# A new work list for a fused attention and SwiGLU kernel: the order of all pieces, the order of the loads, and who masks in the first batches

## The chip, the cores and the metric

The kernel runs on one core of a Trainium2 chip. Its time is the device time of one execution in microseconds; the number that counts is the median of several runs. TensorE (PE) multiplies, VectorE (DVE), ScalarE (ACT) and GpSimd (POOL) work element by element, and 16 DMA engines move data for queues that SP, ACT and GpSimd feed.

## The reference, cut to what matters

```python
# attention: B, H, S, D = 8, 8, 576, 64, and 16 beacon keys ahead of the 576 others
k_all = np.concatenate([beacon_k, k], axis=2)
v_all = np.concatenate([beacon_v, v], axis=2)
scores = 1.0 / np.sqrt(D) * np.matmul(q, k_all.transpose(0, 1, 3, 2))
causal[:, 16:] = np.triu(np.ones((S, S), dtype=bool), k=1)     # beacons are never masked
scores = np.where(causal, -1000000000.0, scores)
a = np.exp(scores - scores.max(-1, keepdims=True))
attn = np.matmul(a / (a.sum(-1, keepdims=True) + 1e-09), v_all)
# feed-forward on the 4608 tokens, 512 wide, 1536 inside
x = attn.transpose(0, 2, 1, 3).reshape(4608, 512)
g = x @ w_gate
out = (g * (1.0 / (1.0 + np.exp(-g))) * (x @ w_val)) @ w_out
```

## The kernel before

The kernel works in bf16 on data that is float32 in memory; loads from GpSimd's queue convert on the way. The order of all work is written out by hand as a string of letters, `plan` (line 615). `piece` (line 560) takes one letter at a time and issues the instructions of the next piece of that kind. As each engine executes its own instructions in the order in which they were issued, the string fixes the order on every engine and in every DMA queue at once, and semaphores hold back a piece whose data or buffer isn't there.

**Attention** goes by batch (8) and pair of heads (4 in a batch, 32 pairs in all). Every pair has four units of scores, A, B, C and D (`UNITS`, line 42), so a batch has 16 units, u0 to u15 for batch 0, u16 to u31 for batch 1 and so on. The letters:

- `S` (`scores`, line 292) multiplies a unit's keys and queries into PSUM: 2 matmuls, 6 for C. `s` is the same with the causal mask added on TensorE by 4 more small matmuls (8 for C) of the matrix `below`.
- `E` (`exponent`, line 323) is the exponent of the unit on ScalarE, from PSUM into the tile `p`.
- `D` and `M` (`mask`, line 330) set the masked part of a unit to zero after the exponent, for units whose scores were issued with `S`: `D` on VectorE by a multiplication, `M` on GpSimd by `affine_select`; one instruction, two for C.
- `P` and `p` (`pv`, line 348) multiply the weights of a pair with the values: 30 matmuls of 64x65 each. `R` (`normalize`) divides by the sums on VectorE and writes `x`.

Queries and keys of batches 0 to 2 come as long runs (`run_loads`) and are turned on TensorE: `c` or `C` regroups on VectorE or ScalarE, `T` transposes on TensorE, `K`/`k` and `Q`/`q` copy the result on VectorE or ScalarE. Those of batches 3 to 7 come in row blocks (`kl`, `ql`), and SP turns them by DMA: `t` is one such transpose (`dma_transposes`, line 272), ten for each batch, alternately of a block of keys and of queries. Values (`vl`) come in six loads a batch. All these tiles exist twice, for even and odd batches; `p` exists three times.

**From attention to the feed-forward part** `x` is transposed to `xT`: for batch 0 on TensorE (`X`, with `Y`/`y` to copy), for the others by five or six DMA transposes of SP (`V`, `x_transpose`, line 392).

**Feed-forward** goes by tiles of 512 tokens (9) and 12 blocks of 128 inner columns. `G` and `H` (`gate_value`, line 404) are 8 matmuls of 64x512 each: the first and second half of gate and value. `g` does the very first block in parts (`parts`, line 557). `a` is a tanh on ScalarE, `1` and `2` are two VectorE instructions that make the gated block. `F` (`project`, line 444) is one step of the output projection, 2 matmuls; `O`/`o` (`evacuate`, line 469) copies 128 finished rows on VectorE or ScalarE and stores them through SP's queue. Weights (`weights`, `load_wo`) are loaded in blocks of columns: `weights[0]` and `[1]` are gate and value for inner blocks 0 to 2, `[2]` and `[3]` for 3 to 5, and so on.

**Buffers and queues.** PSUM is cut into four slots of two banks; each T, S, P, G, X and pair of output blocks takes the next free one (`take`, line 101) and gives it back after its last reader. `l` issues the next load of the list `loads` (line 541) on GpSimd's DMA queue, so loads and `M` masks stand in one line on GpSimd. SP's queue holds `t`, `V` and the stores. `h` orders two idle matmuls (`keep_warm`, line 139) ahead of the next scores or P.

Of the kernel before, what the change touches and what calls it, by code (L numbers as in the profile page):

```python
# [55 lines left out]
def kernel(  # L56
# [112 lines left out]
    def runs(b, src, h0, h1):  # L169
        base = HALF * (src is q)  # L170
        return nc.gpsimd.dma_start(
            qk[b % 2][base : base + HALF, RUN * h0 : RUN * h1].rearrange("p (h e) -> p h e", e=RUN),
            src[b, h0:h1].rearrange("h (p i) d -> p h (i d)", i=ROWS),
        )
# [9 lines left out]
    def q_loads(b):  # L184
        return [lambda c=c, n=n: rows(natural(b, 0), q, b, c, 0, P * c, n) for c, n in enumerate((P, P, P, P, 64))]
# [7 lines left out]
    def k_loads(b):  # L193
        return key_loads(natural(b, 1), k, beacon_k, b)

    def v_loads(b):
        return key_loads(vb[b % 2], v, beacon_v, b)

    def run_loads(b):
        return [lambda: runs(b, k, 0, H), lambda: runs(b, q, 0, H)]  # L200

    def beacon_load(b):
        return nc.gpsimd.dma_start(
            beacons[b][0:NB, :].rearrange("j (h d) -> j h d", d=D), beacon_k[b].rearrange("h j d -> j h d")
        )

    def w_loads(i):
        cols = slice(384 * i, 384 * i + 384)
        return [
            lambda t=t, src=src: nc.gpsimd.dma_start(  # L210
                t[:, :, cols], src[:, cols].rearrange("(kk p) f -> p kk f", p=P)
            )
            for t, src in ((wg, moe_w_gate), (wv, moe_w_val))
        ]

    def load_wo(i):
        fs = slice(6 * i, 6 * i + 6)
        nc.gpsimd.dma_start(wo[:, fs, :], moe_w_out.rearrange("(f p) e -> p f e", p=P)[:, fs, :])
# [53 lines left out]
    def dma_transposes(b):  # L272
        def one(is_k, c, n):
            nc.sync.dma_start_transpose(  # L274
                (qT, kT)[is_k][b % 2][:, :, P * c : P * c + n],
                qk[b % 2][0:n, QK * is_k + H * D * c : QK * is_k + H * D * c + H * D],
            )

        todo = []
        for c in range(NKT):  # L280
            todo.append(lambda c=c: one(1, c, P if c < 4 else 80))
            todo.append(lambda c=c: one(0, c, P if c < 4 else 64))
        return todo
# [246 lines left out]
    for i in range(2):  # L530
# [6 lines left out]
    weights = [load for i in range(4) for load in w_loads(i)]  # L537
    vl = [v_loads(b) for b in range(B)]
    kl = [k_loads(b) for b in range(B)]
    ql = [q_loads(b) for b in range(B)]  # L540
    loads = [
        vl[0][3], vl[0][4], vl[0][1], lambda: beacon_load(1), vl[0][2], vl[0][0], vl[0][5], run_loads(1)[1],
        run_loads(1)[0], weights[0], weights[1], weights[4], weights[2], weights[3], weights[7], vl[1][0],
        vl[1][4], weights[5], run_loads(2)[0], vl[2][0], vl[1][5], vl[1][3], weights[6], vl[1][2], vl[1][1],
        lambda: load_wo(0), lambda: beacon_load(2), lambda: load_wo(1), run_loads(2)[1], ql[3][1], ql[3][4],
        vl[2][4], kl[3][0], kl[3][3], vl[2][1], vl[2][2], kl[3][5], vl[3][2], kl[4][0], ql[3][2], kl[3][2],
        vl[2][5], vl[3][0], vl[2][3], kl[4][2], ql[3][0], vl[3][4], ql[3][3], ql[4][2], kl[4][5], kl[4][3],
        kl[3][1], ql[4][4], vl[3][3], kl[3][4], kl[4][1], ql[4][1], vl[3][1], ql[4][3], kl[4][4], ql[4][0],
        vl[3][5], kl[5][0], kl[5][1], ql[5][0], kl[5][2], ql[5][1], kl[5][3], ql[5][2], kl[5][4], ql[5][3],
        kl[5][5], ql[5][4], vl[4][0], vl[4][1], vl[4][2], vl[4][3], vl[4][4], vl[4][5], kl[6][0], kl[6][1],  # L550
        ql[6][0], kl[6][2], ql[6][1], kl[6][3], ql[6][2], kl[6][4], ql[6][3], kl[6][5], ql[6][4], vl[5][0],
        vl[5][1], vl[5][2], vl[5][3], vl[5][4], vl[5][5], kl[7][0], kl[7][1], ql[7][0], kl[7][2], ql[7][1],
        kl[7][3], ql[7][2], kl[7][4], ql[7][3], kl[7][5], ql[7][4], vl[6][0], vl[6][1], vl[6][2], vl[6][3],
        vl[6][4], vl[6][5], vl[7][0], vl[7][1], vl[7][2], vl[7][3], vl[7][4], vl[7][5],
    ]
    turns = [load for b in range(NPE, B) for load in dma_transposes(b)]
    parts = [(0, [(0, 0), (1, 0), (1, 1), (0, 1)], False), (0, [(0, 2), (1, 2)], False), (0, [(1, 3), (0, 3)], True)]
    wholes = 1

    def piece(kind):  # L560
# [52 lines left out]
    skipped = [0]  # L613

    plan = [
        "0lTlkQlhhhhscEslTKlEsQlEslcEhhscTlKTqlQklEslEsllEsEhshhhhhPlplEsRPEsplXRESEYhhsXEMsYPElscpEcsTRE",
        "TlqKhhPXqKpySlRESgcEMSXclgEYMTgQkMTGaKlqG12SHElDSaGE1H2lGaDl1SHEl2HaDGl1a2G1SHE2HlalG1aM2G1lSHE2",
        "lSaHME1lG2laGD1lSHE2HaDG1a2SHE1lP2alSpDESRMPEp1MSFEFRFFlFFSF2ESMFFFPEMFFpMFlRPFFpcFlFRTFFqFKFVFF",
        "FcFSFOoTESFKFFFEQSFFFcESFFcTFDMElTQFklFSKFEFSlFQFFESMDFFFFMESFMOlGoDlEGlDSHlEGlaDS1HlE2HlaG1Mal2",
        "Gl1SHE2lHlaDG1al2Gl1SHlE2GlaD1Hl2Glat1PlH2tlpaGlRtHl1Gta2H1t2Ga1tSHE2HtaDS1FaFtFE2FFFF1FtSP2EFFD",  # L620
        "ptMSPREFFMtpPRFFtpFRFlSFtESlFFFFlEDSVFFFlFEDSFOFFlFEOSFESlDFFFDFEMSPlFEFpMSFlRFESFEFMFDFSFlESPtF",
        "MFEDlpGtRlGlDtlSHElGtaM1Hlt2Halt1Gal2FFtF1GOoSH2EHaDG1a2G1SHE2HaMlG1al2Gl1SHE2lHlaG1aM2Gl1SHlEt2",
        "GaMtl1SHEl2tHaMSl1FatFFlE2FFFF1tFMSP2EFFtpMSPREFtFpDSlFREStFlFFFEDSlFVFFFEMSFFlFFEDSFloFDPoFlFpE",
        "SFRFESFFFDFEMSFPFEDSpEDSFRtFFESFFDPtEDGDpGRFFFSFEtFlFHDlOoGla1SHlEt2HlaDtGl1a2Glt1SlHE2tHlatGM1a",
        "l2Glt1SHE2tHaDG1ta2Gt1SHE2GaD1SHE2HaDG1a2G1SHE2HaDS1aFFF2EFFF1SFEFF2FFPDFPDppRlSFlEFFFRVSlFESFFD",
        "lFFEDSFFlFFEOSFMoFFFESlFFFMFESMFFFESDPFFEpDSMRPtEFFpDStGREFFMtGSHtEHaDtG1a2FtFH1G2ta1Gt2HGta1Ht2",
        "Ha1Ga2FFF1G2FHOoGa1SHE2MGa1SHE2HaMG1a2G1SHE2HaDS1aFFF2EFFF1SFEFMF2FFPDFPppRlSFlEFFFRVSlFESFFDlFF",
        "ESFFlFFESFloFFFoMDFFMFESFFFFEMSPFEMSpFRFEMSFFEFFDSFMEGGMSHEHaMG1a2FFH1G2a1G2HGa1H2Ha1Ga2FFH1OoGa",
        "2G1SH2EMHa1Ga2G1P2HpaGRH1Ha2S1aFFFEF2FFF1FSF2ESFFDPEDSFpFEDSFESRFFFFESDVFFDFFEDSFFFOFEFFFOFFFDFF",
        "FDFPPppRSFEFFFRSFESFFDPEMSFpFEMRGGDPHpaHRFaFF1VGOoG2H1G2a1H2Ga1H2Ga1H2Ga1H2Ga1H2Ga1H2Ga1H2Ga1FFF",  # L630
        "F2FHGa1H2Ha1Ga2FFH12Ga1G2HGa1FH2Ha1Ga2FFF1G2FHGa1FFFF2FFFFFFFFFoOFFFFFFFFFFFHGa1FFFF2FFFHGa1H2Ha",
        "1Ga2FFF1G2FFHOoGa1H2Ga1FFFF2FFHGa1H2Ha1Ga2FFH12Ga1G2HGa1FFFF2HGa1H2FaFFG1F2FHGa1H2FaFFG1F2FFFFOF",
        "FFFOFFFFFFHGa1H2FaH1FaFF2FFF1FFF2FFFFOFFFFOFFFFFFFFFFFFFFFFFFFFOoFFFFFFFFFFFOFFFFFOFFFFFFFoO",
    ]
    for kind in "".join(plan):
        piece(kind)
# [38 lines left out]
```

## Time and profile before

| | us |
|---|---|
| median of 3 runs | 386.75 (386.39, 386.75, 388.0) |
| the profiled execution | 386.35 |
| its span, first to last instruction | 384.6 |
| TensorE, matmuls busy | 358.7 |
| VectorE busy | 231.5 |
| ScalarE busy | 183.6 |
| GpSimd busy | 123.8 |
| DMA, bytes moved | 39.9 MB |

The span is what lies between the first and the last instruction on the core; the execution's time is 1.75 us more. In the profile's slices each digit is the busy share of one fortieth of the span, 9.6 us. A group of instructions, a line of a timeline or a wait names the engine, the line of the code, the operation and the tiles (out<-in). "Issue" as the end of a wait means that the engine waited for nothing that the profile shows. All matmuls are issued through the helper `halves`, so they carry line 132 and are told apart by their tiles: gv_ps is G and H, o_ps is F, s_ps is S, pv_ps is P and p, t_ps is T, xt_ps is X. GpSimd's masks are line 340, its loads lines 171 to 218; line 274 is `t`, line 397 is `V`.

### The profile page before, as it was taken

To read this page: it belongs to the slowest core of one execution; us is meant where nothing else is said; L and a number is where in the kernel's file an instruction comes from. 1 tells how busy PE (TensorE), PEld (TensorE's weight loads), DVE (VectorE), ACT (ScalarE), POOL (GpSimd) and SP (SyncE) were. 2 spreads that over 40 slices of the span, in tenths; PEclk is the share of its full clock that TensorE was granted. 3 is DMA by queue.
4 is the path that set the end of the run, shared out by engine and by line. 5 is a ranking of instruction groups with operands and counts; after the bars stand their busy time and mean duration, and the time that the engine had idled before them with its cause. 6 is when DMAs were issued, how large, how long until landed. Compare 5 with 4: busy or idle time off the path is not lost.

```text
span 384.6 us, 12123 instructions
## 1 busy us (share of the span) xinstructions
PE 358.7 (93%) x5314; PEld 205.6 (53%) x5314; DVE 231.5 (60%) x424; ACT 183.6 (48%) x266; POOL 123.8 (32%) x200
## 2 busy tenths in 40 slices
PE   6768999999969999679998999999999999999996
PEld 3554556555636456445565556555674555555543
DVE  4473877857834676237863776187737765566552
ACT  2873665663537457526565456734733332232110
POOL 8932663499147386641042004400010000000000
PEclk9896999999989999989999999999999999999999
DMA  8999999899999999999439723901134000110112
GB/s 152 154 204 194 140 201 71 93 201 145 143 116 171 127 162 131 136 164 178 65 34 185 90 70 30 155 3 56 30 91 103 16 2 8 48 56 0 58 56 110
DMA packets 143989, 39.90 MB, mean 104 GB/s; under 512 B 130368, under 2 KB 139328, under 8 KB 143936
## 3 DMA queue, kind: packets, MB, share of 16 engines
q0 software_dynamic: 95424, 18.85, 65.8%
q1 hardware_dynamic: 48224, 19.92, 28.8%
q8 instruction: 41, 0.67, 0.8%
q10 hardware_dynamic: 288, 0.36, 0.3%
q14 instruction: 12, 0.10, 0.1%
HBM read 38.27 MB, written 9.44 MB: 124 GB/s over the span
## 4 chain that ended last, share of the span: by engine, by line
PE 83%; DMA 5%; DVE 4%; issue 4%; ACT 2%; SPq 2%; DVEq 0%
PE gv_ps L132 47%; PE o_ps L132 22%; PE pv_ps L132 7%; PE s_ps L132 6%; DMA xT<-x 2%; DMA first<-in_k_dram 1%; SPq L274 1%; DMA qT<-qk 1%; DVE u L429 1%; DVE o_sb L224 1%; DVE x L373 1%; ACT o_sb L222 1%; DVE turn L224 1%; PE t_ps L130 1%; DVE kT L224 0%
## 5 line engine op out<-in xcount | busy, mean ns | idle before, releaser
L132 PE MATMUL gv_ps<-xT,wg 64*128 64x512 bf16 x864 | 199.6, 377 | 1.7 <-DMA xT<-x 0.7
L132 PE MATMUL gv_ps<-xT,wv 64*128 64x512 bf16 x864 | 200.4, 378 | 0.0
L327 ACT ACTIVATE p<-s_ps 128x992 bf16<-128x992 f32 (+2 forms) x128 | 106.3, 866 | 70.1 <-PE s_ps L132 69.4
L132 PE MATMUL o_ps<-wo,hT 64*128 64x512 bf16 (+2 forms) x912 | 115.7, 370 | 0.2
L132 PEld LDWEIGHTS <-wg 64*128 64x128 bf16 x864 | 80.1, 94 | 45.7 <-PE gv_ps L132 2.6
L429 DVE SCALAR_TENSOR_TENSOR u<-th,gv_ps 128x512 f32<-128x512 f32 x108 | 73.9, 684 | 49.5 <-ACT th L425 49.3
L425 ACT ACTIVATE th<-gv_ps 128x512 f32<-128x512 f32 x108 | 64.4, 596 | 82.4 <-PE gv_ps L132 82.4
L132 PEld LDWEIGHTS <-wv 64*128 64x128 bf16 x864 | 79.7, 94 | 41.4 <-issue 1.5
L436 DVE SCALAR_TENSOR_TENSOR hT<-gv_ps,u 128x512 bf16<-128x512 f32 x108 | 74.6, 691 | 3.6
L340 POOL TENSOR_SCALAR_AFFINE_SELECT p<-p 128x256 bf16<-128x256 bf16 (+2 forms) x65 | 24.8, 398 | 128.2 <-ACT p L327 120.7
L132 PEld LDWEIGHTS <-hT 64*128 64x128 bf16 x912 | 47.4, 95 | 34.3 <-issue 1.4
L132 PE MATMUL s_ps<-qT,kT 64*128 64x80 bf16 (+4 forms) x384 | 46.6, 288 | 7.1 <-DMA qT<-qk 2.4
L132 PE MATMUL pv_ps<-vb,p 64*128 64x65 bf16 x1920 | 41.0, 193 | 9.5 <-issue 9.3
L132 PEld LDWEIGHTS <-p 64*128 64x128 bf16 x1920 | 38.0, 96 | 18.9 <-issue 10.9
L132 PEld LDWEIGHTS <-kT 64*128 64x128 bf16 x384 | 22.6, 96 | 24.9 <-issue 10.8
L180 POOL DMA_DIRECT2D vb<-in_v_dram x40 | 34.3, 869 | 3.5 <-DMA qk<-in_q_dram 1.7
L336 DVE TENSOR_TENSOR p<-p,upper 128x256 bf16<-128x256 bf16 (+2 forms) x77 | 19.7, 276 | 26.0 <-ACT p L327 25.8
L372 DVE RECIPROCAL rec<-pv_ps 128x10 f32<-128x10 f32 x32 | 7.0, 219 | 42.9 <-PE pv_ps L132 42.7
L373 DVE TENSOR_TENSOR x<-pv_ps,rec 128x640 bf16<-128x640 f32 x32 | 26.4, 825 | 1.1
L224 DVE COPY o_sb<-o_ps 128x512 f32<-128x512 f32 (+2 forms) x22 | 14.0, 657 | 16.5 <-PE o_ps L132 13.5
L222 ACT ACTIVATE o_sb<-o_ps 128x512 f32<-128x512 f32 (+1 forms) x16 | 9.0, 580 | 29.8 <-DVE o_sb L224 22.6
L180 POOL DMA_DIRECT2D qk<-in_k_dram x25 | 21.5, 873 | 2.7 <-DMA vb<-in_v_dram 2.4
(52 smaller groups left out, 112.4 us busy)
## 6 DMA issues: line engine op xcount, KB each, us to landing
out_dram<-o_sb SPq DMA_DIRECT2D x34, 256.0 KB, 2.7
vb<-in_v_dram POOLq DMA_DIRECT2D x24, 128.0 KB, 6.6
qk<-in_q_dram POOLq DMA_DIRECT2D x20, 128.0 KB, 7.1
qk<-in_k_dram POOLq DMA_DIRECT2D x15, 128.0 KB, 7.5
wg<-in_moe_w_gate_dram POOLq DMA_DIRECT2D x4, 384.0 KB, 13.4
wv<-in_moe_w_val_dram POOLq DMA_DIRECT2D x4, 384.0 KB, 15.8
wo<-in_moe_w_out_dram POOLq DMA_DIRECT2D x2, 768.0 KB, 11.5
qk<-in_q_dram POOLq DMA_DIRECT2D x2, 576.0 KB, 8.7
```

Of the source, the lines that this page charges most:

```text
L132: ins = nc.tensor.matmul(o, lhsT=l, rhs=r, start=start, stop=stop)
L180: return nc.gpsimd.dma_start(dst[p0 : p0 + n, c, :, 0:D], src[b, :, r : r + n, :].rearrange("h j d -> j h d"))
L222: nc.scalar.activation(o, i, ACT.Copy)
L224: eng.tensor_copy(o, i)
L327: nc.scalar.activation(pt[n // 4 % NPT][:, :, c0 : c0 + w], ps[:, :, 0:w], ACT.Exp, scale=0.125)
L336: nc.vector.tensor_tensor(out=ap, in0=ap, in1=upper[:, None, d : d + w].to_broadcast([P, 2, w]), op=ALU.mult)
L340: nc.gpsimd.affine_select(out=ap, in_=ap, compare_op=ALU.is_ge, fill=0.0, base=d, pattern=[[0, 2], [1, w]], channel_multiplier=-1,)
L372: nc.vector.reciprocal(rec[:], o[:, :, :, D : D + 1])
L373: nc.vector.tensor_tensor(out=xs[b][:, :, P * m : P * m + P].rearrange("p c (h d) -> p h c d", d=D), in0=o[:, :, :, 0:D], in1=rec[:].to_br ...
L425: nc.scalar.activation(th[:], gvs[n][0][:, 0, :], ACT.Tanh, scale=0.5)
L429: nc.vector.scalar_tensor_tensor(out=u[:], in0=ths[n][:], scalar=1.0, in1=gvs[n][0][:, 0, :], op0=ALU.add, op1=ALU.mult)
L436: nc.vector.scalar_tensor_tensor(out=hTs[j][:, f, :], in0=gvs.pop(n)[0][:, 1, :], scalar=0.5, in1=ths.pop(n)[:], op0=ALU.mult, op1=ALU.mult)
```

## The change

Three things are edited; all functions stay as they are.

- `plan` is composed anew. In batches 0 and 1 no unit is masked on GpSimd any more (11 units before): 22 units are masked on TensorE (15 before) and 10 on VectorE (6 before). In later batches 48 units are masked on GpSimd (40 before) and 48 on VectorE (56 before). `h` appears 10 times (16 before). The last scores of batch 3 come earlier against the feed-forward work, those of batches 4 to 7 stand elsewhere too; each kind of feed-forward letter appears as often as before. Two evacuations move from VectorE to ScalarE, and some of the copies `K`, `Q` and `Y` change between the two.
- `loads` is in another order. For batches 3 and 4 keys and queries now come in their natural order, block by block, each batch by itself, then the values of batch 3; before, they were interleaved. In the first part one block of weights comes ahead of the values of batch 0.
- `parts`, the very first gate and value block, is done in two parts (6 and 2 steps) and not three (4, 2 and 2).

The old lines of `loads` and `plan`, which stand in the code above, are left out here.

```diff
@@ -539,22 +539,22 @@
     kl = [k_loads(b) for b in range(B)]
     ql = [q_loads(b) for b in range(B)]
     loads = [
...
+        weights[1], vl[0][2], vl[0][5], vl[0][3], vl[0][0], vl[0][4], vl[0][1], run_loads(1)[1], weights[0],
+        run_loads(1)[0], lambda: beacon_load(1), vl[1][4], weights[3], vl[1][3], weights[2], weights[5],
+        vl[1][1], vl[1][2], weights[4], weights[7], vl[2][0], weights[6], vl[1][5], vl[1][0],
+        lambda: load_wo(1), lambda: load_wo(0), run_loads(2)[1], run_loads(2)[0], lambda: beacon_load(2),
+        vl[2][1], vl[2][2], vl[2][4], vl[2][3], vl[2][5], kl[3][0], kl[3][1], ql[3][0], kl[3][2], ql[3][1],
+        kl[3][3], ql[3][2], kl[3][4], ql[3][3], kl[3][5], ql[3][4], kl[4][0], kl[4][1], ql[4][0], kl[4][2],
+        ql[4][1], kl[4][3], ql[4][2], kl[4][4], ql[4][3], kl[4][5], ql[4][4], vl[3][0], vl[3][1], vl[3][2],
+        vl[3][3], vl[3][4], vl[3][5], kl[5][0], kl[5][1], ql[5][0], kl[5][2], ql[5][1], kl[5][3], ql[5][2],
+        kl[5][4], ql[5][3], kl[5][5], ql[5][4], vl[4][0], vl[4][1], vl[4][2], vl[4][3], vl[4][4], vl[4][5],
+        kl[6][0], kl[6][1], ql[6][0], kl[6][2], ql[6][1], kl[6][3], ql[6][2], kl[6][4], ql[6][3], kl[6][5],
+        ql[6][4], vl[5][0], vl[5][1], vl[5][2], vl[5][3], vl[5][4], vl[5][5], kl[7][0], kl[7][1], ql[7][0],
+        kl[7][2], ql[7][1], kl[7][3], ql[7][2], kl[7][4], ql[7][3], kl[7][5], ql[7][4], vl[6][0], vl[6][1],
+        vl[6][2], vl[6][3], vl[6][4], vl[6][5], vl[7][0], vl[7][1], vl[7][2], vl[7][3], vl[7][4], vl[7][5],
     ]
     turns = [load for b in range(NPE, B) for load in dma_transposes(b)]
-    parts = [(0, [(0, 0), (1, 0), (1, 1), (0, 1)], False), (0, [(0, 2), (1, 2)], False), (0, [(1, 3), (0, 3)], True)]
+    parts = [(0, [(0, 0), (1, 0), (1, 1), (0, 1), (0, 2), (1, 2)], False), (0, [(1, 3), (0, 3)], True)]
     wholes = 1
 
     def piece(kind):
@@ -613,24 +613,24 @@
     skipped = [0]
 
     plan = [
...
+        "0TclqKTlKhslEsQlEsclcTElsKTEslKElhhsQlQEhhslEslEslEslEslhhhhhPElspEsRPESplPREspERsXlEXDXyPyYpgRl",
+        "cXlcyTlcTqgKqTKlGaqKlSHE1G2acslHE1T2aGQklG1lS2HElDGaDSH1E2lSaHDE1G2aGlD1SlHE2HaDlG1al2Gl1SHE2HaD",
+        "G1al2G1SHE2saDPHE12pasRPlEp1SFEF2FFFFRsFEslFFEDSFFPEspEDsFRFlFEFFclPcTplcqTKFFlkFFRTqFlFkFFcVSlq",
+        "FOFFEFlTOFFFKlqSFFEDSlFFFEMSFlFFFEDSlFESDlFPFEMSplFERFSFMtFFlESOGolEGMDtSHMElGtaDlS1HEtl2HaltG1a",
+        "M2Gtl1SHEl2tGlaDl1StHEl2HatMGl1at2Gl1SHE2HlaGM1a2G1SHE2HaDG1a2SHEt1MGa2tP1P2tplpRlSHtElRSaFtlFFE",
+        "1SFlF2FtEFSFlDPDFEDtSlpEDSFRlFtFESFMFPlEtSFpMEDSFltFERSFlFFEFSlFFMDFESVFMFFlFoPlFoFpEMSRFESFlFFF",
+        "DESDFPEFMSplFRFESMFEFFFDlSFDEStPlFFEpltGRlGtlSHEltGal1HVl2Hal1Gal2FFH1l2lGaOloG1MSMH2EMGlaDSt1lH",
+        "E2lHtaGl1at2Gl1MStHE2HaMtG1at2G1SHE2MGa1SHE2HaMG1al2Gl1SHlE2HlaDG1al2Gl1SHlE2HlaG1la2Gl1SlHE2MGa",
+        "D1PH2paGRH1Ga2H12Ga1SHE2HaDG1a2G1SHE2HaDS1aFFF2EFFF1SFEtFMF2FFMFPtFFpStRFESFFFFtEDSFFFFEMSFtFOFF",
+        "oFFDFEFFDFFtFFPPtppRSlFtEFFlFRSFEStlFFFFElSFVFFFlEOSFoFPlESFMpMFERSMFFFESFDFFDPDEMSFDEpSFRFEMSFF",
+        "FESDtFFFFPEMtFDGptGRHtGat1H2Hta1Gat2FFH1o2GatOG1SH2EtGaDtS1HE2HtaMG1a2G1SHE2HaMG1a2G1SHE2GaD1SHE",
+        "2HaMS1FaFFE2FFFF1FSF2ESFFFDPEDFFMpSRlFESFlFFFVEDSlFFFFEDlSFFFFoOlFFDPElFDFpSRFESFFFFEDSPFEFMpSFR",
+        "FEMSFEFFDFSFMEGGMSHEHaMG1a2FFH1G2a1G2FHOGOa1SHE2MGa1FFFF2FFHGa1H2Ha1Ga2FFH12Ga1G2HGa1FFFF2HFaFH1",
+        "FaF2FFF1FFF2FFFOFFFFOPPppRSFEFFFRSFMESFFVPEDSFpFEDSFMESRFFFFEMSFFFFEDSFFOFFoFPDESFDEpSFRFEMSFFFE",
+        "SDFFPFEDGMpGRHGa1H2Ha1Ga2FFH12Ga1G2HGa1FFFF2FFFPFFpoOHRGaV1H2Ga1H2Ga1FH2Ha1Ga2FFF1G2HHa1Ga2FFH12",
+        "Ga1G2HGa1H2Ha1Ga2FFH12Ga1G2HGa1H2Ha1Ga2FFF1G2FHGa1FFFF2FFFFFFFFFOHOFaFFG1F2FFFFFFFHGa1FFFF2FFFFF",
+        "FFFFoOFFFFFFHGa1H2Ha1Ga2FFF1G2FFHGa1H2Ha1Ga2FFH12Ga1G2FFFFFHGa1H2Ha1Ga2FFF1G2FFHooGaFF1FFF2FFFFF",
+        "FFHFaFH1FaF2FFF1FFF2FFFoFFFoFFFFFFFFFFFFFFFFFFFFFOFFOFFFFFFFFFoFFFFoFFFFFFFFoO",
     ]
     for kind in "".join(plan):
         piece(kind)
```

More of the change, by code (lines that the diff above doesn't have):

```diff
@@ L541 @@
     loads = [
[L542 to L551, printed above, removed]
@@ L552 @@
-        vl[5][1], vl[5][2], vl[5][3], vl[5][4], vl[5][5], kl[7][0], kl[7][1], ql[7][0], kl[7][2], ql[7][1],
-        kl[7][3], ql[7][2], kl[7][4], ql[7][3], kl[7][5], ql[7][4], vl[6][0], vl[6][1], vl[6][2], vl[6][3],
-        vl[6][4], vl[6][5], vl[7][0], vl[7][1], vl[7][2], vl[7][3], vl[7][4], vl[7][5],
+        weights[1], vl[0][2], vl[0][5], vl[0][3], vl[0][0], vl[0][4], vl[0][1], run_loads(1)[1], weights[0],
+        run_loads(1)[0], lambda: beacon_load(1), vl[1][4], weights[3], vl[1][3], weights[2], weights[5],
@@ L615 @@
     plan = [
[L616 to L630, printed above, removed]
@@ L631 @@
-        "F2FHGa1H2Ha1Ga2FFH12Ga1G2HGa1FH2Ha1Ga2FFF1G2FHGa1FFFF2FFFFFFFFFoOFFFFFFFFFFFHGa1FFFF2FFFHGa1H2Ha",
-        "1Ga2FFF1G2FFHOoGa1H2Ga1FFFF2FFHGa1H2Ha1Ga2FFH12Ga1G2HGa1FFFF2HGa1H2FaFFG1F2FHGa1H2FaFFG1F2FFFFOF",
-        "FFFOFFFFFFHGa1H2FaH1FaFF2FFF1FFF2FFFFOFFFFOFFFFFFFFFFFFFFFFFFFFOoFFFFFFFFFFFOFFFFFOFFFFFFFoO",
+        "0TclqKTlKhslEsQlEsclcTElsKTEslKElhhsQlQEhhslEslEslEslEslhhhhhPElspEsRPESplPREspERsXlEXDXyPyYpgRl",
+        "cXlcyTlcTqgKqTKlGaqKlSHE1G2acslHE1T2aGQklG1lS2HElDGaDSH1E2lSaHDE1G2aGlD1SlHE2HaDlG1al2Gl1SHE2HaD",
```

## The prediction

> **What bounds the kernel now.** I read the page's part 1, the slices, the chain of waits, then TensorE's timeline at every dip of its row.
>
> ```profile
> span 384.6 us, 12123 instructions
> PE 358.7 (93%) x5314; PEld 205.6 (53%) x5314; DVE 231.5 (60%) x424; ACT 183.6 (48%) x266; POOL 123.8 (32%) x200
> PE   6768999999969999679998999999999999999996
> PE 83%; DMA 5%; DVE 4%; issue 4%; ACT 2%; SPq 2%; DVEq 0%
> q8 instruction: 41, 0.67, 0.8%
> ```
>
> TensorE is the bound, and what can be won is in the dips, all but one before 210 us. To size them I give each item of the work list its full-clock spacing in the timeline: a G or H 0.864 us, an F 0.216, a P or p 0.45, four scores of a pair 0.70, a T 0.26, an X 0.36, a matmul of keep_warm 0.107. The 1,724 letters come to 344.0 us of "work time", counted from the first T at 6.89 us. An item's start less its work time is its lag: 6.9 at first, 20.2 at the first G (38.42 us), 39.1 at the end. Where it grows, by TensorE's timeline (start, length, item, and in brackets its idle time and what ended it):
>
> ```profile
> 30.38 0.92 PE L132 MATMUL pv_ps<-vb,p 64*128 64x65 bf16 x27 [3.51 <-issue]
> 108.29 0.39 PE L132 MATMUL s_ps<-qT,kT 64*128 64x496 bf16 x2 [0.70 <-DMA kT<-qk]
> 111.31 0.57 PE L132 MATMUL s_ps<-qT,kT 64*128 64x464 bf16 x2 [2.42 <-DMA qT<-qk]
> 157.31 0.29 PE L132 MATMUL pv_ps<-vb,p 64*128 64x65 bf16 x7 [1.82 <-issue]
> 165.43 0.20 PE L132 MATMUL pv_ps<-vb,p 64*128 64x65 bf16 x1 [3.60 <-issue]
> ```
>
> And three stretches of the view by windows (length, then busy time of PE, weight loads, DVE, ACT, POOL; then the granted clock, the DMA share and GB/s):
>
> ```profile
> 30.40:36.20 5.80, 5.66 (x81) 2.87 (x81) 2.37 (x4) 2.48 (x3) 1.34 (x3) 0.50 1.48 196
> 111.30:114.70 3.40, 3.39 (x22) 1.54 (x24) 0.29 (x1) 1.61 (x2) 0.00 (x0) 0.50 1.95 146
> 166.00:169.30 3.30, 3.30 (x50) 2.06 (x47) 1.64 (x5) 1.87 (x2) 2.19 (x3) 0.50 1.41 242
> ```
>
> The clock is 0.50 after each stop of about 3 us. So the first stop costs 3.5 + 2.9, the one at 108 to 111 (batch 3's scores wait for their transposes) 0.9 + 2.6 + 1.7, the last 3.6 + 1.7. The rest: 2.0 at 157; 1.3 at 131 and 1.0 at 71.5 for a PSUM slot; 1.5 at 207 (xT).
>
> The three "issue" stops are not data. TensorE's 10,628 matmuls and weight loads over 256 give 41.5, and q8 has 41 packets of 16 KB: they are its instructions, 256 a block. The trace has one of them from 28.10 to 29.06, 154.50 to 155.71 and 162.76 to 163.93, each before the end of such a stop, and the last two stops are exactly 256 instructions apart. Counting from there, every block was fetched when the block ahead of it began, and was ready about 1.5 us after the packet's end: 3.6 to 4.2 us in all with loads alone (38 to 67 us), 6.0 to 6.4 with transposes beside them (112, 128), 7.3 to 8.1 beside an x transpose (149 to 165, 206). A block of G, H or F lasts 13.8 us and hides it; a P and a p are 120 instructions in 0.9 us.
>
> **The skill.** "Runtime: NRT & Kernel Launch", section "Instruction fetch mechanics", has refills of 256 instructions, fetched while the current block runs and mostly hidden; it gives TensorE room for eight blocks, and says two lines elsewhere. The trace agrees on 256 and behaves as with two; not hidden, at 3.60 us. "TensorE: Matmul & The Clock Gate", section "What's actually happening", halves the clock after an idle window of some 3.4 us; the three rows at 0.50 agree. The forecast goes by the trace.
>
> **The change, part by part.**
>
> *Masks.* In batches 0 and 1 GpSimd loses 15 affine_selects. Their busy time (15 x 398 ns) hides nothing; their place did, for loads stand behind them while they wait for an exponent:
>
> ```profile
> POOL p L340 <- ACT p L327: 120.7, 30, 21.1
> 34.42 0.37 POOL L340 TENSOR_SCALAR_AFFINE_SELECT p<-p 128x224 bf16<-128x224 bf16 x1 [5.78 <-ACT p L327]
> 49.18 0.68 POOL L340 TENSOR_SCALAR_AFFINE_SELECT p<-p 128x256 bf16<-128x256 bf16 x2 [4.71 <-ACT p L327]
> 20.99 0.55 POOL L180 DMA_DIRECT2D vb<-in_beacon_v_dram  x1 [2.53 <-DMA qk<-in_q_dram]
> ```
>
> The first line is from the waits, the rest from GpSimd's timeline. The last shows its other gate: a load is issued when the eighth load before it has landed (here Q of batch 1, at 20.70; the next two, 23.93 and 25.81, follow landings at 23.65 and 25.52). Without masks the queue feeds DMA without a break until the first M (work time 51.7, some 73 us): batch 3's last K and Q can go out at about 65 us (the last weights and Q, K of batch 2 landed by 58, eleven loads at 0.9 alongside and after); before, the last went out at 88.85. Seven more scores are masked on TensorE, +1.0 us of work; 12 fewer keep_warm matmuls, -1.3: together -0.3. VectorE has 13 mask instructions in batches 0 and 1 instead of 7. From the first G to H of unit 10 (21.5 us) it then holds 11 x (684 + 691 ns), seven masks 2.25, three copies 2.24, 33 gaps of 0.05: 21.3 us. It just fits; 0 to 1.5, I take 0.7. From batch 2 on, M goes from 40 to 48 pieces, on an idle engine.
>
> *Start.* The joined g (6 steps, then 2) is the same matmuls; the copies and two evacuations that change between VectorE and ScalarE (0.75 against 0.65 us, 657 against 580 ns) are counted at nothing, as they come where the other has room. ScalarE now runs 16 exponents almost back to back (13.4 us from about 9.6), so P of pair 2 could come at 20.6, with V landed at 17.6 (one weight load ahead of it, +2). But P begins a block (work 6.9) at 18.3, and the next (9.5) is 2.6 us on; a fetch of 5.0, as at 18.9 before, stops TensorE 2.7 us. The block after (3.1 us, then ready 6 to 7 us after 23.3) stops it 3.2 us more, with a half clock after (2.9). With P of pair 3, two g, an X and three T at that clock the first G comes about 36.5, at work 15.7: lag 20.8, against 20.2. Bounds: -2 (fetches at 4) to +3 (a second drop). Weights land 5 us or more ahead of their G by the landings of before (2 us a block, 4 a wo).
>
> *Loads in order, transposes early.* Times in work time. Batch 3's ten transposes begin at 55.5 (69.9 before) and end at 68.1; first score 79.1: 11.0 us of slack where there were 3.2. SP issues one per 1.3 us and it lands in 8 at worst: the stop at 108 to 111 goes, -5.2. What is late next: batch 4's transposes (76.4 to 86.8, first scores 94.7 and 95.8). 13 us of issue and 7.9 to land make 97.3, 1.5 late; the fetch stops below push those scores further, so it is not added. Behind them on SP stand the x transposes of batch 2: five issues of 1.45 us from about 90, the fourth landed near 100, for a G at 97.8 plus the same stops: nothing. x of batch 3 moves from 123.8 to 102.2, 17.7 ahead of its G (8.9 before). V of batch 3 lands by about 80 for its P at 85.2: from 51.7 the queues hold 14.5 full loads, 15 transposes and four outputs, at 0.85, 0.95 and 0.7 us (estimates: 12 loads' worth landed between 86.6 and 96.5 us, and nine loads with seven transposes between 122.8 and 138). Masks M behind loads: the mask of u62 stands behind the load that waits for kl[5][4]; by the 12.6 us that the six loads from 105.6 took, that lands at about 94 and P needs the mask at 96.4: nothing, and 1 to 2 us if it slips.
>
> *The crowded stretch.* Batch 3's attention, 79 to 98 instead of 85 to 122, puts four short blocks in a row (5.0, 5.6, 4.8, 5.0 us of work from 78.4) among loads, batch 4's transposes and x of batch 2. At 6.0, 6.0, 6.4, 6.4 for a fetch that is 1.0 + 0.4 + 1.6 + 1.4 = 4.4. ScalarE has 19 exponents at 0.86 and two evacuations, 17.6 of 18.7 us: +1.0 (0 to 2). One half clock: 1.7. Sum 7.1. From 152.4 three more (4.0, 5.2, 5.2) lie at batch 5's transposes and x of batch 4: at 5.5, 6.4, 5.5 that is 3.0; the xT wait of 207 hides in it. Between them blocks of G and H: the stops at 157 and 165 are gone, -7.3.
>
> *Sum.* Lag: 20.8, + 0.7, + 0.9 for a PSUM slot as at 71.5, + 7.1, + 0.5 for another, + 3.0, + 1.2 for the last third as before = 34.2, against 39.1. With -0.3 the span is 379.4 and the execution 381.15 (the profiled one is 386.35, 1.75 over its span); the median shown, 386.75, is 0.4 above that, so 381.5.
>
> **Rivals.** 0.5% either way (384.8 to 388.7) is about what can be told from no change.
> - *Quiet fetches.* Without load and x traffic on top of each other a fetch takes 4.5: of the seven blocks only the one of 4.0 stops, 0.5, no clock drop. Lag 20.8 + 0.7 + 0.9 + 1.0 + 0.5 + 0.5 + 1.2 = 25.6: 372.9. For: loads run ahead. Against: 53 us of transfers, by the sizes above, are placed at 76 to 116.
> - *The plan does not do what it says:* the start takes most of its upper bound (+2.4) and batch 4's scores wait as batch 3's did (+2.6): 386.5.
> - *Slower, by instruction fetch* in those seven blocks. At 7.3 us, as at 206, they stop 8.8 and 7.5 us, with a drop in each stretch (1.7): lag 44.8, time 392. It turns at 6.7 us a fetch. For: 7.3 to 8.1 was measured beside x transposes. Against: at 112 and 128 it was 6.0 to 6.4.
>
> **Chances.** Forecast 0.48 (its own range 376 to 384.7), quiet fetches 0.14, no change 0.16, slower 0.22. Faster 0.62, within 0.5% 0.16, slower 0.22. Half of the first rival lies under 374 and half of the last over 391: range 374 to 391.
>
> **What would show it.** Right: no wait on qT or kT at u48; GpSimd's row full to 60 us; the waits named "issue" at the second and third pair of the start and near 100 to 130 us, 1 to 2 us each, none at 155 to 165; VectorE over nine tenths at 40 to 58 us. Wrong: "issue" under 3 us in all after the start (then 373), or over 15 us (then 392); a score of batch 4 waiting over 3 us for qT; a P waiting for a GpSimd mask.

## The result, and the profile after

The changed kernel takes 391.94 us (median of 18 runs, 387.71 to 395.92), the kernel before 388.01 in the same session (18 runs, 385.92 to 389.37): **1.0088 times the time, interval 1.0061 to 1.0115**. It is slower; the forecast was 381.5, and 391.94 lies beyond its range too. (Medians are of all runs, ratios of runs in the chip's fast state alone, so a ratio is not quite the quotient of two medians.) It comes nearest to the third rival, "slower, by instruction fetch", which had named 392: that its total fits is in part luck, as the part on why tells. The profiled execution took 392.0 us, its span 389.5 (384.6 before).

The page of the changed kernel, the same lines as those shown of before, and the row of the granted clock:

```profile
span 389.5 us, 12163 instructions
PE 360.5 (93%) x5338; PEld 206.5 (53%) x5338; DVE 227.9 (59%) x413; ACT 186.0 (48%) x271; POOL 122.7 (31%) x197
PE   6659999999977689999998999999999999999996
PEclk9885999999998989999999999999999999999999
PE 82%; DMA 6%; issue 4%; POOL 3%; DVE 2%; SPq 2%; ACT 1%; POOLq 0%
q8 instruction: 41, 0.67, 0.8%
```

The busy shares and the chain's shares by engine have hardly moved; they tell nothing. The row of slices does: counted from 0, before had its dips behind the start in slices 11 (6) and 16 and 17 (6, 7); now 16 and 17 are full and there is one long dip, 7, 7, 6, 8, in slices 11 to 14 (107 to 146 us). The start is a little worse. TensorE's timeline names the stops, each line the first work after one:

```profile
20.06 0.62 PE L132 MATMUL pv_ps<-vb,p 64*128 64x65 bf16 x30 [2.17 <-DMA vb<-in_v_dram]
26.56 0.65 PE L132 MATMUL pv_ps<-vb,p 64*128 64x65 bf16 x17 [3.45 <-issue]
32.76 0.57 PE L132 MATMUL pv_ps<-vb,p 64*128 64x65 bf16 x14 [0.68 <-issue]
...
108.20 0.37 PE L132 MATMUL s_ps<-qT,kT 64*128 64x464 bf16 x2 [1.27 <-DMA qT<-qk]
113.14 0.40 PE L132 MATMUL pv_ps<-vb,p 64*128 64x65 bf16 x15 [1.41 <-issue]
121.71 1.89 PE L132 MATMUL o_ps<-wo,hT 64*128 64x512 bf16 x7 [2.58 <-issue]
129.27 0.62 PE L132 MATMUL pv_ps<-vb,p 64*128 64x65 bf16 x29 [1.00 <-issue]
138.19 0.37 PE L132 MATMUL gv_ps<-xT,wg 64*128 64x512 bf16 x1 [3.96 <-issue]
```

The last four stops are the crowded stretch of the prediction, batch 3's attention. They are 256 instructions apart, the last one nearly (the trace has 255, 256 and 251 matmuls and weight loads between them), and a packet of q8 ends 1.3 to 1.4 us before the end of each (111.84, 120.30, 127.89, 136.79 us). A block that is left by such a stop was entered at the end of the stop before, and the next block was asked for then. So the distances between the lines from 113.14 on are the fetch times themselves: 8.57, 7.56, 8.92 us; the first, from the block's entry at about 105.0, is 8.2. (The line at 108.20 is another thing, a score that waits for its transpose.) The forecast had 6.0, 6.0, 6.4 and 6.4 and called 6.7 the turning point. The Trainium skill's sentence on refills ("Runtime: NRT & Kernel Launch", "Instruction fetch mechanics") that they are mostly hidden does not hold in this stretch: 8.95 us of stops in a row are theirs.

In the view by windows (columns as before), the start's stretch at half clock, and the two that follow the long stops:

```profile
25.90:39.50 13.60, 11.93 (x207) 7.61 (x208) 5.48 (x11) 4.44 (x7) 6.61 (x9) 0.50 1.55 193
121.40:124.80 3.40, 3.09 (x41) 1.91 (x43) 0.00 (x0) 0.00 (x0) 2.48 (x4) 0.50 1.88 153
138.50:141.90 3.40, 3.40 (x21) 1.47 (x18) 0.00 (x0) 0.67 (x2) 1.54 (x2) 0.50 1.92 153
```

By lags (start less work time, as in the prediction) the profiled run divides as follows; predicted in brackets: 24.0 at the first G (20.8); + 2.5 to 83 us (2.1: VectorE and two slots); + 14.9 over the stretch, 83 to 151 us (7.1); + 1.9 from there to 210 us, the xT wait of 1.5 among it (3.0); + 1.3 to 380 us (1.2). That is 44.6 for 34.2, and before 39.4 at the same work.

### The profile page after: what moved, and what is told of

Same layout as the page of the kernel before. It is cut to its first block, busy times and chain, and to the rows that moved or that the text cites. A ratio compares the mean times of both kernels' runs of the same rounds, so it can differ in the third digit from the quotient of the medians.

```text
span 389.5 us, 12163 instructions
## 1 busy us (share of the span) xinstructions
PE 360.5 (93%) x5338; PEld 206.5 (53%) x5338; DVE 227.9 (59%) x413; ACT 186.0 (48%) x271; POOL 122.7 (31%) x197
## 4 chain that ended last, share of the span: by engine, by line
PE 82%; DMA 6%; issue 4%; POOL 3%; DVE 2%; SPq 2%; ACT 1%; POOLq 0%
PE gv_ps L132 45%; PE o_ps L132 23%; PE pv_ps L132 7%; PE s_ps L132 5%; DMA qT<-qk 2%; DMA vb<-in_v_dram 2%; DMA xT<-x 2%; SPq L274 1%; POOL vb L180 1%; DVE o_sb L224 1%; PE t_ps L130 1%; PE xt_ps L386 1%; POOL qk L171 1%; SPq L397 1%; ACT o_sb L222 0%
## 5 line engine op out<-in xcount | busy, mean ns | idle before, releaser
L132 PE MATMUL gv_ps<-xT,wg 64*128 64x512 bf16 x864 | 201.9, 380 | 6.5 <-issue 4.0
L132 PE MATMUL gv_ps<-xT,wv 64*128 64x512 bf16 x864 | 203.3, 380 | 0.0
L340 POOL TENSOR_SCALAR_AFFINE_SELECT p<-p 128x256 bf16<-128x256 bf16 (+2 forms) x62 | 23.3, 396 | 116.9 <-ACT p L327 100.3
L132 PEld LDWEIGHTS <-p 64*128 64x128 bf16 x1920 | 38.8, 96 | 18.1 <-issue 7.6
L224 DVE COPY o_sb<-o_ps 128x512 f32<-128x512 f32 (+1 forms) x20 | 12.9, 666 | 20.4 <-PE o_ps L132 10.5
L180 POOL DMA_DIRECT2D qk<-in_q_dram x25 | 21.6, 864 | 3.8 <-DMA vb<-in_v_dram 2.9
## 6 DMA issues: line engine op xcount, KB each, us to landing
vb<-in_v_dram POOLq DMA_DIRECT2D x24, 128.0 KB, 10.6
```

Of the source, the lines that this page charges most:

```text
L132: ins = nc.tensor.matmul(o, lhsT=l, rhs=r, start=start, stop=stop)
L180: return nc.gpsimd.dma_start(dst[p0 : p0 + n, c, :, 0:D], src[b, :, r : r + n, :].rearrange("h j d -> j h d"))
L224: eng.tensor_copy(o, i)
L340: nc.gpsimd.affine_select(out=ap, in_=ap, compare_op=ALU.is_ge, fill=0.0, base=d, pattern=[[0, 2], [1, w]], channel_multiplier=-1,)
```

## The experiments

Each kernel is compared with the kernel before, run on the same chip in turn with it; that ratio is the number to use, as the absolute times of one kernel wander by some us. For the changed kernel the ratio is 1.0088.

### Which half: the start or the rest

Two kernels join one half of each list and its loads at the end of batch 1's attention (the last `p` of batch 1).

```diff
# start_old: list and loads of before up to the last p of batch 1, the changed ones from there
# start_new: the changed ones up to there, those of before after it
```

> The work list and loads of the kernel before up to the last p of batch 1, then those of the changed kernel for all that is left. If the loss of the start (lag 24.0 us at the first G against 20.2) is the list's own, this runs about 3.8 us under the changed kernel, near 388 us; the stops by instruction fetch between 110 and 140 us stay. If the start's loss is chance of that one profile, it stays at 392.

> The other way round: the changed kernel up to the last p of batch 1, then the list and loads of the kernel before. The list's own start: about 3.8 us over the kernel before, near 392 us, with the stops at 106 to 111 and 155 to 165 us of before still there. Chance: 388 us. If losses of the two parts add up, this and the run with the old start together come to 780 us.

Measured: start_old 385.45 us, ratio 0.9999 (0.9973 to 1.0025); start_new 389.53, ratio 1.0062 (1.0031 to 1.0093). So the start of the changed list costs 0.6% (start_new against before) to 0.9% (changed against start_old), some 2.4 to 3.5 us, and the rest of it is worth nothing by itself, though it holds everything from which I had expected a gain. TensorE's timeline of start_old shows why:

```profile
112.08 0.30 PE L132 MATMUL s_ps<-qT,kT 64*128 64x336 bf16 x3 [1.52 <-issue]
120.57 0.38 PE L132 MATMUL pv_ps<-vb,p 64*128 64x65 bf16 x13 [2.72 <-issue]
128.14 0.26 PE L132 MATMUL pv_ps<-vb,p 64*128 64x65 bf16 x5 [1.55 <-issue]
137.46 0.39 PE L132 MATMUL gv_ps<-xT,wg 64*128 64x512 bf16 x1 [2.26 <-issue]
```

Again four stops, at other pieces of work, since this list has 48 instructions fewer ahead of them and its blocks are cut elsewhere: they belong to the stretch, not to a piece. And start_new has the late stops of before (165.72 us, 3.26 us of issue). The changed list takes the old stops away and puts four in their place.

### Take the transfers out of the stretch

Theory: a fetch takes 8 us there because loads, transposes of batch 5 and an x transpose go on at the same time. The kernel "relieved" leaves every piece of computing in its order and moves transfers only: 45 loads (the 63rd to the 107th), batch 5's ten transposes and the x transpose of batch 3 to later places in the list, the loads from work time 97.5 on.

```diff
-"...G1SHE2HaDG1a2SHEt1MGa2tP1P2tplpRlSHtElRSaFtlFFE",
-"1SFlF2FtEFSFlDPDFEDtSlpEDSFRlFtFESFMFPlEtSFpMEDSFltFERSFlFFEFSlFFMDFESVFMFFlFoPlFoFpEMSRFESFlFFF",
+"...G1SHE2HaDG1a2SHEt1MGa2tP1P2tppRSHtERSaFtFFE1SFF",
+"2FtEFSFDPDFEDtSpEDSFRFtFESFMFPEtSFpMEDSFtFERSFFFEFSFFMDFESVFMFFFoPFoFpEMSRFESFFFFDESDFPEFMSpFRFE",
```

> The changed kernel with 45 loads, ten transposes of batch 5 and the x transposes of batch 3 moved out of the stretch in which batch 3's attention runs, to places up to 50 us of work later, all still ahead of their need. Instruction fetch held up by transfers: a fetch there takes 4 to 5 us and no longer 6.5 to 9, so the four stops of 1.4, 2.6, 1.0 and 4.0 us and the half clocks behind them go: 8 to 10 us less, about 383 us. ScalarE as the bound of that stretch, or late data: the same 392 us within 1.5, as its work and its data's order stay.

Measured: 380.68 us, ratio 0.9828 (0.9777 to 0.9879), **2.6% less than the changed kernel's ratio, about 10 us**, without one piece of computing moved. The profiled span is 377.2. All of TensorE's stops of over 0.9 us from 15 to 200 us, in its timeline:

```profile
21.29 1.01 PE L132 MATMUL pv_ps<-vb,p 64*128 64x65 bf16 x30 [2.08 <-DMA vb<-in_v_dram]
28.95 0.65 PE L132 MATMUL pv_ps<-vb,p 64*128 64x65 bf16 x17 [3.38 <-issue]
107.24 0.37 PE L132 MATMUL s_ps<-qT,kT 64*128 64x464 bf16 x2 [1.19 <-DMA qT<-qk]
191.36 0.34 PE L132 MATMUL pv_ps<-vb,p 64*128 64x65 bf16 x11 [1.16 <-issue]
```

The four are gone; the start is as in the changed kernel. The last line is new, and not free: the transfers that were moved now meet later attention, and stops named issue of 0.69, 1.16 and 0.63 us stand at 184, 191 and 233 us, where the changed kernel has none over 0.6. The same window in both kernels, first the changed one:

```profile
112.00:125.00 13.00, 9.29 (x175) 5.54 (x176) 3.07 (x7) 7.07 (x10) 7.73 (x13) 0.87 1.97 132
```

```profile
112.00:125.00 13.00, 13.00 (x349) 8.19 (x344) 4.83 (x14) 11.51 (x16) 5.73 (x13) 1.00 0.48 77
```

The DMA share (next to last; it adds up the time of all packets over that of 16 engines, so it can pass 1) falls from 1.97 to 0.48, and TensorE is busy all the time. The fetches of the same blocks, from the entry of a block to 1.4 us after the end of its q8 packet (108.41, 112.67, 117.20 and 122.74 us), take 5.7, 3.5, 2.4 and 3.1 us in place of 8.2, 8.6, 7.6 and 8.9. ScalarE is busy for 11.51 of 13.00 us and stops nothing.

### Make the blocks longer instead

The other side of the same theory: leave the transfers and take instructions out. P and p are 30 matmuls over 64 rows each; over all 128 rows they are 15, with the same sums.

```diff
+                hh = int(second)
+                halves(("p", n), hh, 2, o_ps[:, hh, 68*c : 68*c+D+1],
+                    pt[n % NPT][:, hh, col : col + P], vb[b % 2][:, t, 2*m+hh, 0 : D+1],
+                    c == 0 and t == 0, c == t == NKT - 1)
```

> The changed kernel with P and p as 15 matmuls over 128 rows each and not 30 over 64: 60 instructions for a pair and not 120, so that a block of 256 lasts longer wherever attention is dense. Instruction fetch as the cause: the stops of the start and of the crowded stretch shrink by 5 to 10 us; what a matmul of 128 rows and 65 columns costs is not in any trace (0.45 us for 15 if two halves ran side by side before, up to 0.9 if not, so 0 to 14 us for 32 pairs of P and p). Any other cause: only that cost shows, and the stops stay where they were.

Measured: 381.98 us, ratio 0.9861 (0.9805 to 0.9918). Its page, and the longest of its waits for data in the stretch:

```profile
PE 363.6 (96%) x4378; PEld 194.5 (51%) x4378; DVE 228.3 (60%) x413; ACT 186.1 (49%) x271; POOL 122.2 (32%) x197
PE   7689999999898899999999999999999999999996
PE 84%; DMA 7%; SPq 4%; POOL 3%; DVE 1%; issue 1%; ACT 0%; POOLq 0%
q8 instruction: 34, 0.56, 0.6%
```

```profile
125.31 0.37 PE L132 MATMUL gv_ps<-xT,wg 64*128 64x512 bf16 x1 [2.75 <-DMA xT<-x]
```

Seven packets fewer, every stop of 0.9 us or more named issue gone, and no transfer moved in the list. What then comes late is data: xT by 2.75 us. Such a P takes the same 0.44 us, but about 0.11 us goes at each change between matmuls over half and over all rows (start to start 308 ns into such a P for 196 before, 125 out of it for 15). The trace has 52 changes each way, some 11 us by this estimate, so the stops and what hung on them were worth about twice the net gain.

The two experiments change different sides of one comparison (fetch time against a block's length), and each removes the stops. Instruction fetch as the cause of the stops in the stretch, and of the loss that hangs on them, is shown.

### Give the masks back to GpSimd

Rival: what changed is who masks in the first two batches. The ten `D` of batches 0 and 1 are made `M`, in place; the seven further units masked on TensorE are left as changed. One of the three lines of the edit:

```diff
-"...SHE1G2acslHE1T2aGQklG1lS2HElDGaDSH1E2lSaHDE1G2aGlD1SlHE2HaDlG1al2Gl1SHE2HaD",
+"...SHE1G2acslHE1T2aGQklG1lS2HElMGaMSH1E2lSaHME1G2aGlM1SlHE2HaMlG1al2Gl1SHE2HaM",
```

> The changed kernel with the ten units of batches 0 and 1 that VectorE masks given to GpSimd again, nothing moved. If taking the masks off GpSimd is what feeds the loads without a break, they go out later by GpSimd's waits for exponents (4 to 6 us each before), batch 3 runs later against its data and the time changes by 2 us or more, either way; if loads have slack enough at those places, 392 us within 1.5.

Measured: 391.79 us, ratio 1.0115 (1.0071 to 1.0158), against 1.0088 (1.0061 to 1.0115): no difference that these runs can tell. The stops of the stretch remain, with 3.33 us at 131.90. Who masks these ten units explains neither the loss nor a gain of more than about half a per cent; the seven units on TensorE were not tried.

### Use GpSimd's wait ahead of the first M

The trace after has GpSimd idle in the middle of its loads. Its timeline, and the window (DMA share and GB/s at the end):

```profile
64.16 0.79 POOL L180 DMA_DIRECT2D qk<-in_k_dram  x1
77.42 0.40 POOL L340 TENSOR_SCALAR_AFFINE_SELECT p<-p 128x256 bf16<-128x256 bf16 x1 [12.48 <-ACT p L327]
```

```profile
65.00:77.00 12.00, 11.92 (x306) 7.33 (x302) 9.01 (x19) 8.90 (x14) 0.00 (x0) 1.00 0.61 54
```

The first `M` of batch 2 waits 12.48 us for its exponent while loads stand behind it in the list, and DMA moves 54 GB/s, where the start's window has 193. The kernel "early_v3" issues seven loads (the last queries and the values of batch 3) ahead of that mask.

```diff
-        kl[3][3], ql[3][2], kl[3][4], ql[3][3], kl[3][5], ql[3][4], kl[4][0], kl[4][1], ql[4][0], kl[4][2],
+        kl[3][3], ql[3][2], kl[3][4], ql[3][3], kl[3][5], ql[3][4], vl[3][0], vl[3][1], vl[3][2], vl[3][3],
+        vl[3][4], vl[3][5], kl[4][0], kl[4][1], ql[4][0], kl[4][2], ql[4][1], kl[4][3], ql[4][2], kl[4][4],
...
-        "FOFFEFlTOFFFKlqSFFEDSlFFFEMS...
+        "FOFFEFlTOFFFKlqSFlllllllFEDSlFFFEMS...
```

> The changed kernel with the six value loads of batch 3 and one query load moved ahead of the first GpSimd mask of batch 2, that is into the 12 us from 65 to 77 us in which GpSimd waits for an exponent and DMA stands nearly still. If the stops between 110 and 140 us come from transfers piled up there, seven loads fewer (6 us of transfers) shorten the four fetches: 2 to 4 us less, 388 to 390 us. If the pile at 80 to 110 us plays no part: 392 us.

Measured: 388.35 us, ratio 1.0033 (1.0005 to 1.0061): about 2 us less than the changed kernel's ratio, at the low edge of what was expected, and the intervals just touch. That seven of 45 loads out of the way are some of it is likely, then, but not shown; they are not all of it.

### The start: values ahead of the weights

The first stop of the start waits for values that landed at 20.01 us, 2.4 us later than I had said; one block of weights had been put ahead of them.

```diff
-        weights[1], vl[0][2], vl[0][5], vl[0][3], vl[0][0], vl[0][4], vl[0][1], run_loads(1)[1], weights[0],
+        vl[0][2], vl[0][5], vl[0][3], vl[0][0], vl[0][4], vl[0][1], weights[1], run_loads(1)[1], weights[0],
```

> The changed kernel with the first weight load behind the six value loads of batch 0, where the kernel before has it. P of pair 0 stood still from 17.6 to 20.1 us in the changed kernel; if it waits for values that the weight load made late, the stop shrinks by about 2 us. The time falls by 1.5 to 2.5 us if that is on the path, and by less than 1 us if the instruction fetch behind it (ready at 26.5 us) sets the end of the start anyway.

> The changed kernel itself, beside the next two on one chip: ratio to before 1.006 to 1.012 as measured. A second profile of it tells whether the stops fall at the same instructions: if a block's fetch causes them, the same edges (every 256 instructions) stop again, with other lengths.

Measured: v_first 390.18 us, ratio 1.0117 (1.0061 to 1.0174); the changed kernel again 390.78 (383.69 to 394.23, six runs), for 386.39 of before. **A miss**: 1.5 to 2.5 us less were expected and none shows. TensorE's timeline of v_first:

```profile
25.29 0.53 PE L132 MATMUL pv_ps<-vb,p 64*128 64x65 bf16 x17 [2.46 <-issue]
31.48 0.39 PE L132 MATMUL pv_ps<-vb,p 64*128 64x65 bf16 x14 [1.41 <-issue]
110.13 0.40 PE L132 MATMUL pv_ps<-vb,p 64*128 64x65 bf16 x15 [1.95 <-issue]
```

The wait for values is gone, and the first G comes at a lag of 22.0 instead of 24.0. But changed_again, with the weights in front, also had 22.0 in its profile. Two single profiles of one kernel differ by as much as the edit should bring; the fetch stops behind the wait stay in all three. How the loss of the start divides between the values and the fetches is left open; the next runs bear on it.

### The kernel before with longer blocks, and the combinations

If short blocks cost the kernel before its first stop and those of 157 and 165 us, P and p over all rows in batches 0 and 4 alone should help it too.

```diff
+                if b in (0, 4):      # before_whole;  b == 0 in relieved_whole0 and best
+                    ...              # the four lines above
+                    continue
```

> The kernel before with P and p of batches 0 and 4 alone as 15 matmuls over 128 rows. The prediction took the stops at 27, 155 and 162 us for instruction fetch (6.4 + 2.0 + 5.3 us with their half clocks). If so they go and 16 P and p pay about 0.2 us each at the change of row mode, as in the run with all of them whole: 387 - 13.7 + 3.3, about 377 us. If they are late values or another cause, 387 to 390 us.

> The kernel with moved transfers, and P and p of batch 0 as 15 matmuls over 128 rows. Instruction fetch at the start: its first G comes at a lag of about 18 us and not 24.4, as with all P and p whole, so 380.7 - 6 us = 374 to 375 us. If the gain of the whole P and p lay in the crowded stretch alone: 381 us.

> All that the runs point to together: start and loads of the kernel before up to the last p of batch 1, then the changed list with the transfers moved out of the crowded stretch, and P and p of batch 0 over 128 rows. Lag at the first G 14.5 us (18.0 with the changed start): 377.0 - 3.5 = 373.5 us, ratio to before about 0.965. If the start's gain is lost to a later wait: 377 us.

Measured: before_whole 382.42 us, ratio 0.9865 (0.9824 to 0.9905); 377 was expected. Its first G came at a lag of 14.5, six less, of the stops named issue at 157 and 165 us one of 0.94 us is left (at 154), but two stops in its timeline are new or larger than before:

```profile
60.30 0.32 PE L132 MATMUL pv_ps<-vb,p 64*128 64x65 bf16 x9 [1.90 <-issue]
...
108.81 0.57 PE L132 MATMUL s_ps<-qT,kT 64*128 64x464 bf16 x2 [2.72 <-DMA qT<-qk]
```

With fewer instructions ahead of them, all later block edges fall elsewhere: one now falls among P's at 60 us. And a TensorE that is earlier waits longer for the transposes of batch 3.

relieved_whole0 is "relieved" with batch 0's P and p over all rows: 376.97 us, ratio **0.9686** (0.9627 to 0.9745), where 374 to 375 us was expected. best has the start of before, the rest of relieved and the same P and p: 376.18 us, ratio 0.9771 (0.9723 to 0.9819), where 0.965 was expected; another miss. It has the earlier first G (lag 16.05 for 18.0) and gives it back:

```profile
61.53 0.32 PE L132 MATMUL pv_ps<-vb,p 64*128 64x65 bf16 x9 [1.57 <-issue]
78.62 0.37 PE L132 MATMUL gv_ps<-xT,wg 64*128 64x512 bf16 x1 [1.46 <-DMA xT<-x]
189.76 0.61 PE L132 MATMUL pv_ps<-vb,p 64*128 64x65 bf16 x29 [2.37 <-issue]
```

Which of the two is faster these runs do not tell, as their intervals overlap. The lowest ratio is that of the changed order with its transfers spread out and fewer instructions in batch 0: 2.6% to 3.7% less than before by the interval.

These lags say something of the start, too. With P and p of batch 0 over all rows no stop of over 0.6 us named issue is left there in either list, and yet the first G comes at 18.0 in the changed list (relieved_whole0) and at 14.5 and 16.05 in the old one. So some 2 to 3.5 us of the start's loss is not instruction fetch. The wait for values, 1.90 us in relieved_whole0 and absent in before_whole, may be the larger part; no pair of runs isolates it.

## Why the prediction was wrong

**What held.** The mechanism, the place and some of the sizes: stops named issue at block edges of 256 instructions, at the start and at 105 to 138 us; none at 155 to 165 any more; the stop at 108 to 111 smaller, 1.3 us for 3.1, though not gone; the xT wait of 207; the last third (1.3 for 1.2).

**The step that failed: "At 6.0, 6.0, 6.4, 6.4 for a fetch that is 1.0 + 0.4 + 1.6 + 1.4 = 4.4."** I took fetch times from 112 and 128 us of the kernel before, where loads and transposes ran, and used them for a stretch into which my own list of transfers put loads, two kinds of transposes and stores. They were 8.2, 8.6, 7.6 and 8.9. A stop is a fetch less a block, so some 2.1 us more on each of four fetches would turn 4.4 us of stops into 12.9; they added 9.7 of lag, as the wait for a transpose and the half clock made the blocks longer; two drops of the clock follow (2.1 by the lag) where I had counted one (1.7), and batch 3's second scores wait 1.4. With 1.7 in steps too small to name the stretch comes to 14.9. The figure that comes near was in the prediction: 7.3 to 8.1, measured beside an x transpose, and I gave it to a rival.

The rival's 392 is partly luck. It had 20.8 at the first G, 11.5 in the stretch and 9.2 behind it; measured are 24.0, 14.9 and 1.9. A start and a stretch that were worse and a second group that had no such stop cancel.

**"11.0 us of slack" for batch 3's transposes, "one per 1.3 us".** SP's timeline has them from 81.71 us on, some of them at twice that:

```profile
85.06 2.34 SPq L274 DMA_TRANSPOSE qT<-qk  x1
87.49 2.19 SPq L274 DMA_TRANSPOSE kT<-qk  x1
...
99.52 1.24 SPq L274 DMA_TRANSPOSE qT<-qk  x1
```

Ten took 19 us, two stores of 1.08 us in all among them, not 13, and the last one landed at 108.07. The slack went, and 1.3 us more.

**"GpSimd's row full to 60 us", "feeds DMA without a break until the first M".** The page has, one digit for 9.7 us:

```profile
POOL 8754526095664747550171015200100000000000
DMA  8999999399999999990799618910330400110112
```

GpSimd's row was not full; that of DMA was, to about 65 us, as GpSimd's loads wait for earlier ones to land (1.57 us at 57.25, for one). What the prediction left out is what the first `M` does to the loads behind it. It held them for 12.5 us, and they went out later, ahead of and into the stretch. Removing a mask from the queue moved the wait to the next mask, as the kernel before has waits of 4.7 and 5.8 us at its own. Values took 10.6 us from issue to landing (median), for 6.6 before.

**The start, "lag 20.8".** It was 24.0. The values landed at 20.0, not 17.6. The first fetch took 6.1 us, not 5.0, and stopped 3.45, not 2.7; the second took 6.2 and stopped 0.68 us, not 3.2, as its block ran at half clock and so covered more. That half clock is what I had short: 13.6 us of it, from 25.9 to 39.5, where I had one drop of 5.8.

**Terms that were too high.** VectorE was to be "over nine tenths" busy at 40 to 58 us:

```profile
40.00:58.00 18.00, 17.69 (x193) 9.20 (x191) 15.10 (x29) 12.16 (x19) 6.99 (x10) 1.00 1.70 190
```

It is 15.10 of 18.00, 84%; the lag grew by 0.6 there, for 0.7 predicted, so the sum came out by luck: the engine was not as full as I had it. ScalarE's 1.0 in the stretch was nothing (relieved keeps its exponents and has no such stop). The second group was 1.9 for 3.0, and most of it is the xT wait (1.5), not a fetch.

**A sign that misled.** I wrote that issue of over 15 us after the start would mean 392. It was 9.0 us, and the time was 392 all the same: what hangs on the stops (clock drops, a late transpose, steps of a few tenths) and the start were not in that figure.

**Left open.** The time of one execution of the changed kernel lies anywhere from 383.7 to 395.9 us. Two profiles have the same four edges and fetch times of 8.2, 8.6, 7.6, 8.9 and 7.5, 9.1, 7.8, 8.7. What makes a fetch long no run here separates by an edit of its own, as relieved moved loads and transposes together. Its trace says more than that, though. SP's timeline, then GpSimd's on both sides of a stretch without a load:

```profile
115.10 8.05 SPq L397 DMA_TRANSPOSE xT<-x  x5
```

```profile
97.41 0.42 POOL L340 TENSOR_SCALAR_AFFINE_SELECT p<-p 128x256 bf16<-128x256 bf16 x1
122.27 0.54 POOL L180 DMA_DIRECT2D qk<-in_beacon_k_dram  x1
```

Batch 4's transposes and those of x kept their places (SP issues them almost without a pause up to 123.15), GpSimd issued no load from 97.4 to 122.3, and the fetches from 110.6 on took 3.5, 2.4 and 3.1 us. From 125.8 us, with loads and no transpose being issued, one took 6.0. In the changed kernel, with both, they took 7.6 to 8.9. So transposes alone did not make a fetch long here, and the loads are the likelier part. Which of the 45 loads matter is not shown.

## What to carry to other kernels

When a stop is named issue, count instructions between stops and look at the instruction queue's packets: if stops are whole blocks apart, TensorE waits for its own code, and a stop is the fetch time less the time of one block. Then two levers are open, both worth about 10 us here: keep transfers away from the short blocks, or put fewer instructions into them. And a load list is judged by what stands between the loads: an instruction that waits on the issuing engine can turn "early" loads into a late burst (12.5 us later here; what that alone costs is not shown).

## What the hardware showed unexpectedly

- A fetch of 256 TensorE instructions took from 2.4 us (relieved, near 116 us, DMA share 0.44) to 8.9 us (changed kernel, 129 to 138 us, DMA share 1.64).
- Fewer instructions for the same products: 15 matmuls over 128 rows take the same 0.44 us as 30 over 64, and about 0.11 us more at each change of rows. It was still 10 us faster over the kernel (ratio 0.9861 against 1.0088).
- Issuing one DMA transpose on SP took 1.2 to 2.6 us in the same kernel. The long ones stand mostly among loads (85 to 89 us), but relieved has one of 1.90 at 101.75 with no load being issued; the cause is not shown.
- A half clock of 13.6 us (25.9 to 39.5) followed stops of 3.45 and 0.68 us; in the second profile of the same kernel, after 3.55 and 0.68 us at the same places, it lasted 6.8 (25.5 to 32.3). So these two stops alone do not set how long it holds. Nor does it take a stop of 3.4 us: it came after 2.58 us in the changed kernel, and the prediction's middle row at 0.50 stands after 2.42 us, with 0.70 shortly before.
